# Batch 1 of a fused attention and GELU kernel: v loaded in three lots, a different split of the second GEMM, and the last head pair masked by matmuls

## Chip, cores and metric

The kernel runs on one core of a Trainium2 chip. The metric is the device time of one execution in microseconds (us), the median of the runs shown. In the profile PE is TensorE (matmul), PEld its weight loads, DVE VectorE, ACT ScalarE, POOL GpSimd and SP SyncE, which here only issues transfers.

## What is computed

For 8 batches of 8 heads, with 576 tokens and a head size of 64, the kernel computes causal attention with a decay taken from f, and passes the result through two GEMMs with an exact GELU between them. Cut to what matters, the reference is:

```
scores = scale * q @ k.T
cum    = cumsum(log(clip(f, 1e-4, 1)))
attn   = softmax(where(causal, -1e9, scores + cum[:, None] - cum[None, :]))
x      = (attn @ v) as [4608 tokens, 512]
out    = gelu(x @ w_in[512, 2048]) @ w_out[2048, 512]
```

The inputs are float32 in memory; the transfers that POOL issues turn q, k, w_in and w_out into bf16 on their way.

## The kernel before

One batch is one stage. Its attention handles four head pairs (`HP = 4`), and each pair four score tiles, `scores(b, i, t)` for t = 0 to 3 (L280). A tile is made by PE in one of two PSUM buffers (`s_psum`), turned into `e` by an exponential on ACT (L310), and then its diagonal blocks are made causal. There are two ways for that. With `on_pe` false, POOL writes zeros with an `affine_select` (L312), after the exponential. With `on_pe` true, PE adds a large negative number beforehand by small matmuls of two constants, `key_of` and `after` (L300). Batch 0 and pair 0 of batch 1 go by PE, all others by POOL. Then `attend` (L324) multiplies `e` with the weighted v, `normalize` (L339) divides on DVE, and after transposes to `xT` the first GEMM of this batch (`gemm1`, L381) runs over 16 blocks of d_ff with a GELU on ACT for each (L406).

The second GEMM of batch b lies inside the attention of batch b + 1: it is a generator of single steps, and `take(fill, n)` draws n of them between the attention's instructions on PE. A step for one of 16 blocks kt of d_ff is either one matmul over all 128 rows ("n") or two over 64 rows each into two PSUM banks ("r"), which DVE adds later. For batch 0 there are two parts. `gemm2_first` (L510), 16 steps, lies in the attention of batch 1: token blocks 0 and 1 with kt 0 to 7, so with the first half of w_out. The rest lies in the attention of batch 2: `gemm2_second` (L533) for the same blocks with kt 8 to 15, then `PLAN_0` (L452) for token blocks 2 and 3 with all kt, then batch 1's own second GEMM (`PLAN_1`). PSUM banks come from three pools of two buffers each, "s" for scores, "o" for attention results and transposes, "m" for GEMMs.

There is no scheduler: every engine works its instructions in the order of the program text. So the place of a call sets its place in each engine's queue, that of a transfer too. What matters here:

- POOL issues the transfers of q, k (L108), w_in (L172) and w_out (L176) and also computes: selects (L312), the weighted v (`weigh_v`, L269 and L276), and the copies `behind` and `gate` (L573, L568), which read a tile that a transfer fills and so hold POOL, and all transfers behind it, until that has landed.
- SP issues v (L120), the transposing transfers of q and k for batches 2 and on (`transpose_dma`, L236), those of x (L370), and the stores (L506). A small `memset` of v_sb on POOL ahead of a load of v holds the load until POOL is there.
- w_out comes in four quarters of four kt each (`load_w_out(0)` to `(3)`).

In batch 1, `second_attention` (L721) writes out the order by hand: q and k of pairs 1 to 3 are transposed by PE (`transposes`, L730, and DVE copies L217) right after the first two score tiles, and v of batch 1 comes in two lots of four heads. v and q, k of batch 2 are loaded during batch 1; DVE puts the transposed q and k in their places (`untangle`, L241) during batch 1's first GEMM.

The functions that the diff touches, with the profile's line numbers:

Of the kernel before, what the change touches and what calls it, by code (L numbers as in the profile page):

```python
# [9 lines left out]
FP32 = mybir.dt.float32  # L10
BF16 = mybir.dt.bfloat16
Act = mybir.ActivationFunctionType
Alu = mybir.AluOpType
PSUM = bass.MemoryType.PSUM

P = 128
# [37 lines left out]
def kernel(  # L54
# [223 lines left out]
    e_of = {}  # L278

    def scores(b, i, t):  # L280
        on_pe = b == 0 or (b == 1 and i == 0)
        st = s_psum.tile([P, 2, 512], FP32, tag="s", name=f"s{t}")
        c = 0
        for n, q0, w in STILES[t]:
# [164 lines left out]
        (3, "s", 16 * "n"),  # L449
    ]  # L450

    PLAN_0 = [(2, "o", 16 * "r"), (3, "m", 14 * "r" + 2 * "n")]  # L452
    PLAN_1 = [
        (0, "m", 14 * "r" + 2 * "n"),
        (1, "m", 14 * "r" + 2 * "n"),
# [53 lines left out]

    def gemm2_first(c):  # L510

        pss = [
            m_psum.tile([P, d_model], FP32, tag="m", name="ps2") for _ in range(2)
        ]
        for kq in (0, 4):
            for ts in range(2):
                for kt in range(kq, kq + 4):
                    nc.tensor.matmul(  # L518
                        pss[ts],
                        g_of[c][kt][:, ts * P : (ts + 1) * P],  # L520
                        w_out_sb[:, kt, :],
                        start=(kt == 0),
                        stop=(kt == 7),
                    )
                    if kt == 7:
                        ot_of.append(
                            o_pool.tile([P, d_model], FP32, tag="ot", name="ot")
                        )
                        copy = nc.scalar.copy if ts else nc.vector.tensor_copy
                        copy(ot_of[ts], pss[ts])  # L530
                    yield

    def gemm2_second(c):  # L533

        for ts, pool, tag in ((0, o_psum, "o"), (1, m_psum, "m")):
            banks = [
                pool.tile([P, d_model], FP32, tag=tag, name="ps2") for _ in range(2)
            ]
            for kt in range(8, n_ff):
                for r in range(2):  # L540
                    rows = slice(r * D, (r + 1) * D)
                    nc.tensor.matmul(  # L542
                        banks[r],
                        g_of[c][kt][rows, ts * P : (ts + 1) * P],
                        w_out_sb[rows, kt, :],
                        start=(kt == 8),
                        stop=(kt == n_ff - 1),
                    )
                if kt == n_ff - 1:
                    nc.vector.tensor_tensor(ot_of[ts], ot_of[ts], banks[1], Alu.add)  # L550
                    sum_out(c, ts, ot_of[ts], banks[0])
                yield

    def gemm2_third():
        yield from gemm2_second(0)
        yield from gemm2_rows(0, PLAN_0)
        yield from gemm2_rows(1, PLAN_1)

    def take(gen, n):
# [15 lines left out]
    def first_attention():  # L575
# [45 lines left out]
        weigh_v(0, 3)  # L621
        load_w_in(2)
        nc.gpsimd.memset(v_sb[:, :, 0, 0:1], 0.0)
        load_v(1, 0, 4)
        load_w_in(3)
        load_qk_tokens(1, 0, 4)
        load_qk_tokens(1, 4, 8)
# [93 lines left out]
    def second_attention():  # L721


        b, fill = 1, gemm2_first(0)

        def av(i, h):
            attend(b, i, h, (0, 1, 2, 3, 4))
            normalize(b, i, h)

        def transposes(i, pool, tag):  # L730
            for which in range(2):
                transposes_first(b, i, which, pool, tag)


        nc.scalar.activation(warm[0:1, 0:1], warm[0:1, 0:1], Act.Exp)
        def tiles(i, t):
            scores(b, i, t)
            scores(b, i, t + 1)

        def run(i):  # L740
            av(i, 0)
            av(i, 1)

        tiles(0, 0)
        transposes(1, o_psum, "o")
        transposes(2, m_psum, "m")
        transposes(3, o_psum, "o")
        tiles(0, 2)
        take(fill, 2)
        tiles(1, 0)  # L750
        run(0)
        tiles(1, 2)
        take(fill, 4)
        weigh_v(1, 2)
        tiles(2, 0)
        run(1)
        weigh_v(1, 3)
        tiles(2, 2)
        take(fill, 4)
        tiles(3, 0)  # L760
        transpose_dma(2, 0, 4)
        transpose_dma(2, 4, 8)
        to_xT(b, 0, nc.vector.tensor_copy, o_psum, "o")
        to_xT(b, 1, nc.vector.tensor_copy, o_psum, "o")
        take(fill, 2)
        tiles(3, 2)
        behind(qk_of[2][1], H - 1)
        load_w_out(2)
        load_w_out(3)
        run(2)  # L770
        take(fill, 4)
        av(3, 0)
        both = s_psum.tile([P, 2, 1024], BF16, tag="s", name="ps_x2")
        to_xT(b, 2, nc.scalar.copy, ps=both[:, 0, 0:XC])
        av(3, 1)
        gemm1_begin(1, both)
        x_tail(1)
        load_v(2)

    for b in range(B):  # L780
# [8 lines left out]
        for ffb in range(4 if b < 2 else 5, n_ff):  # L789
            gemm1(b, ffb, ps=spare() if b > 1 and ffb in (7, 8) else None)  # L790
            if b == 0:
# [2 lines left out]
                        transposes_first(1, 0, which, o_psum, "o")  # L794
                if ffb == 12:
                    behind(qk_of[1][0], H - 1)
                    nc.gpsimd.memset(v_sb[:, 4:8, 0, 0:1], 0.0)
                    load_v(1, 4, 8)
                    weigh_v(1, 0)
                    load_w_out(1)  # L800
                    weigh_v(1, 1)
                    load_qk_tokens(2)
            elif b + 1 < B:
                first, gap = (5, 3) if b == 1 else (1, 4)
                at, late = divmod(ffb - first, gap)
# [40 lines left out]
```

## Time and profile before

| what | value |
|---|---|
| median of 5 runs | 337.94 us (337.22 to 340.28) |
| the profiled execution's own time | 339.24 us |
| its span, first to last instruction | 337.1 us |
| time outside the span | 2.1 us |
| PE busy | 324.0 us, 96% of the span |
| ACT busy | 209.3 us, 62% |
| DVE busy | 181.1 us, 54% |
| POOL busy | 122.6 us, 36% |
| granted TensorE clock | 0.995 of full |
| attention of batch 1, by the timeline | 40.6 to 57.5 us |
| first GEMM of batch 1, by the timeline | 57.6 to 72.0 us |
| attention of batch 2, by the timeline | 72.0 to 103.4 us |

Times in windows and timelines are in us from the start of the span. A timeline row gives start, length, engine, line, operation, output and inputs, and in brackets the idle time of the engine ahead of it with what ended it. A windows row gives the stretch, its length, then for PE, PEld, DVE, ACT and POOL the busy time with the number of instructions, the granted clock, the busy share of the 16 DMA engines (packets can overlap, so that it can pass 1), and GB/s. In the DMA view, a queue's row gives its packets, MB, and the time its packets took as a share of the 16 engines: q0 carries the transfers that POOL issues, q1 those of SP.

### The profile page before, as it was taken

To read this page: it belongs to the slowest core of one execution; us is meant where nothing else is said; L and a number is where in the kernel's file an instruction comes from. 1 tells how busy PE (TensorE), PEld (TensorE's weight loads), DVE (VectorE), ACT (ScalarE), POOL (GpSimd) and SP (SyncE) were. 2 spreads that over 40 slices of the span, in tenths; PEclk is the share of its full clock that TensorE was granted. 3 is DMA by queue.
4 is the path that set the end of the run, shared out by engine and by line. 5 is a ranking of instruction groups with operands and counts; after the bars stand their busy time and mean duration, and the time that the engine had idled before them with its cause. 6 is when DMAs were issued, how large, how long until landed. Compare 5 with 4: busy or idle time off the path is not lost.

```text
span 337.1 us, 7780 instructions
## 1 busy us (share of the span) xinstructions
PE 324.0 (96%) x3121; PEld 172.3 (51%) x3161; DVE 181.1 (54%) x414; ACT 209.3 (62%) x299; POOL 122.6 (36%) x250
## 2 busy tenths in 40 slices
PE   8699989999999999999999999999999999999995
PEld 3584555445554456445654555446544654444443
DVE  4761265674466945895479547964696540020011
ACT  6967698673653788278927982788368855404600
POOL 8191098009436134633554243724361420000000
PEclk9989999999999999999999999999999999999999
DMA  7999999997998989697958697599810241011013
GB/s 116 183 137 185 196 190 171 153 182 144 210 221 181 138 167 202 120 140 130 211 148 128 123 198 150 94 151 210 146 56 2 82 61 64 0 63 64 0 39 86
DMA packets 104627, 44.16 MB, mean 131 GB/s; under 512 B 83408, under 2 KB 100048, under 8 KB 104592
## 3 DMA queue, kind: packets, MB, share of 16 engines
q1 hardware_dynamic: 87296, 29.52, 45.9%
q0 software_dynamic: 16896, 13.63, 27.9%
q8 instruction: 24, 0.39, 0.5%
q10 hardware_dynamic: 400, 0.52, 0.4%
q14 instruction: 11, 0.09, 0.1%
HBM read 36.85 MB, written 9.44 MB: 137 GB/s over the span
## 4 chain that ended last, share of the span: by engine, by line
PE 90%; issue 2%; SPq 2%; DVE 1%; POOL 1%; ACT 1%; DMA 1%; POOLq 0%; ACTq 0%; DVEq 0%
PE ps L386 36%; PE ps L482 26%; PE o L331 10%; PE ps L422 8%; PE s L300 7%; SPq L120 2%; ACT e L310 1%; PE ps L542 1%; DMA v_sb<-in_v_dram 1%; POOL q L108 1%; PE ps_x L364 1%; PE ps L518 0%; POOL k L108 0%; DVE qT L217 0%; DVE kT L217 0%
## 5 line engine op out<-in xcount | busy, mean ns | idle before, releaser
L406 ACT ACTIVATE g<-ps 128x512 bf16<-128x512 f32 x144 | 82.1, 601 | 83.6 <-PE ps L386 83.6
L310 ACT ACTIVATE e<-s 128x896 bf16<-128x896 f32 (+2 forms) x128 | 100.2, 835 | 22.7 <-PE s L300 17.5
L386 PE MATMUL ps<-xT,w_in_sb 128*128 128x512 bf16 x497 | 111.5, 379 | 0.7
L482 PE MATMUL ps<-w_out_sb,g 64*128 64x512 bf16 (+1 forms) x692 | 104.4, 376 | 1.6 <-issue 1.3
L386 PEld LDWEIGHTS <-w_in_sb 128*128 128x128 bf16 x576 | 56.0, 98 | 67.5 <-issue 1.8
L312 POOL TENSOR_SCALAR_AFFINE_SELECT e<-e 128x256 bf16<-128x256 bf16 (+1 forms) x135 | 49.1, 383 | 86.1 <-ACT e L310 85.7
L482 PEld LDWEIGHTS <-g 64*128 64x128 bf16 (+1 forms) x711 | 39.4, 95 | 34.8 <-issue 4.2
L269 POOL TENSOR_TENSOR vw<-v_sb,wT 128x640 bf16<-128x640 f32 x30 | 38.6, 1289 | 27.6 <-DMA v_sb<-in_v_dram 15.4
L300 PE MATMUL s<-qT,kT 64*128 64x320 bf16 (+4 forms) x384 | 44.2, 278 | 2.9 <-ACT e L310 1.9
L250 DVE COPY kT<-tk 64x288 bf16<-64x288 bf16 x96 | 43.9, 457 | 1.6
L250 DVE COPY qT<-tq 64x288 bf16<-64x288 bf16 x96 | 38.7, 403 | 5.1 <-DMA tq<-q 3.7
L331 PE MATMUL o<-vw,e 128*128 128x65 bf16 x960 | 38.1, 195 | 2.0 <-DVE vw L269 1.2
L331 PEld LDWEIGHTS <-e 128*128 128x128 bf16 x960 | 35.1, 99 | 9.4 <-issue 2.7
L490 DVE COPY ot<-ps 128x512 f32<-128x512 f32 x20 | 13.8, 692 | 47.1 <-PE ps L482 47.1
L345 DVE TENSOR_TENSOR x<-o,r 128x320 bf16<-128x320 f32 x64 | 31.4, 491 | 3.6 <-DMA xT<-x 1.4
L300 PEld LDWEIGHTS <-kT 64*128 64x128 bf16 x384 | 19.8, 94 | 24.6 <-issue 8.1
L431 DVE COPY ot<-ps 128x512 f32<-128x512 f32 (+2 forms) x9 | 5.7, 632 | 49.6 <-PE ps L422 49.6
L422 PE MATMUL ps<-w_out_sb,g 128*128 128x512 bf16 (+2 forms) x142 | 27.9, 355 | 0.1
L422 PEld LDWEIGHTS <-g 128*128 128x128 bf16 x144 | 13.5, 98 | 14.5
L344 DVE RECIPROCAL r<-o 128x5 f32<-128x5 f32 x64 | 12.1, 189 | 13.3 <-PE o L331 13.2
L502 DVE TENSOR_TENSOR ot<-ot,ps 128x512 f32<-128x512 f32 x22 | 15.1, 685 | 1.1
L386 PE MATMUL ps<-tails,w_in_sb 128*128 128x512 bf16 x63 | 14.2, 377 | 0.1
(69 smaller groups left out, 138.3 us busy)
## 6 DMA issues: line engine op xcount, KB each, us to landing
out_dram<-ot SPq DMA_DIRECT2D x32, 256.0 KB, 2.5
v_sb<-in_v_dram SPq DMA_DIRECT2D x24, 256.0 KB, 4.9
q<-in_q_dram POOLq DMA_DIRECT2D x6, 576.0 KB, 6.4
k<-in_k_dram POOLq DMA_DIRECT2D x6, 576.0 KB, 8.5
v_sb<-in_v_dram SPq DMA_DIRECT2D x22, 128.0 KB, 4.8
w_in_sb<-in_moe_w_in_dram POOLq DMA_DIRECT2D x4, 512.0 KB, 8.4
w_out_sb<-in_moe_w_out_dram POOLq DMA_DIRECT2D x4, 512.0 KB, 10.0
q<-in_q_dram POOLq DMA_DIRECT2D x4, 144.0 KB, 4.0
```

What stands on the lines that cost most here:

```text
L250: nc.vector.tensor_copy(rows[:, odd], src[odd * D : (odd + 1) * D, 2 * i + h].rearrange("d j p -> d p j"),)
L269: eng.tensor_tensor(vw(b)[:, hs, :, 0:D], v_sb[:, hs, :, :], w.unsqueeze(3).to_broadcast([P, 2, NBLK, D]), Alu.mult,)
L300: nc.tensor.matmul(to, *ab, start=half < 0, stop=half == 1 or not masked)
L310: nc.scalar.activation(et[:, :, z:c], st[:, :, z:c], Act.Exp, scale=scale)
L312: nc.gpsimd.affine_select(out=et[:, :, c0 + z : c0 + P], in_=et[:, :, c0 + z : c0 + P], compare_op=Alu.is_ge, fill=0.0, base=z, pattern=[[ ...
L331: nc.tensor.matmul(o[:, m, :], e_of[b, i, t][:, h, c : c + P], vw_of[b][:, 2 * i + h, n, :], start=(n == 0), stop=(n == m),)
L345: nc.vector.tensor_tensor(x_of[b, i][:, :, h, :], o[:, :, 0:D], r.unsqueeze(2).to_broadcast([P, NBLK, D]), Alu.mult,)
L386: nc.tensor.matmul(ps, w_in_sb[:, kt, ffb * P : (ffb + 1) * P], src[:, kt, 0:TC], start=(kt == 0), stop=(kt == n_dm - 1),)
L406: nc.scalar.activation(g_of[c][ffb], ps, Act.Gelu)
L422: nc.tensor.matmul(pss[ts][:, c0:c1], g_of[c][kt][:, ts * P : (ts + 1) * P], w_out_sb[:, kt, c0:c1], start=(kt == 0), stop=(kt == n_ff - 1),)
L482: nc.tensor.matmul(banks[r], g_of[c][kt][rows, ts * P : (ts + 1) * P], w_out_sb[rows, kt, :], start=kt == (steps.index("r") if r else 0), ...
L502: nc.vector.tensor_tensor(ot, ot, bank, Alu.add)
```

## The change

It touches batch 1 and what lies around it, in five places.

1. v of batch 1 comes in three lots: heads 0 and 1 early, in the place of heads 0 to 3, and heads 2 and 3, then 4 to 7, behind the gate on q.
2. The transfer of k for batch 2 goes from the first GEMM of batch 0 to the attention of batch 1, and that of w_out's second quarter to a place behind the gate on that k, where quarters 2 and 3 are already.
3. `gemm2_first` takes all four token blocks with kt 0 to 3, so with w_out's first quarter alone; `gemm2_second` takes the other 12 kt of all four blocks, and `PLAN_0` is gone. The number of steps stays 16 in batch 1 and 112 in batch 2.
4. Pair 3 of batch 1 is masked by PE.
5. In batch 1's attention the transposes of pairs 1 and 2 change their PSUM pools, two steps of the second GEMM go ahead of score tiles 2 and 3 of pair 0, the transposes of pair 3 behind these, and two steps fewer are drawn ahead of pair 3's `attend`.

```diff
--- before.py
+++ after.py
@@ -278,7 +278,7 @@
     e_of = {}
 
     def scores(b, i, t):
-        on_pe = b == 0 or (b == 1 and i == 0)
+        on_pe = b == 0 or (b == 1 and i in (0, HP - 1))
         st = s_psum.tile([P, 2, 512], FP32, tag="s", name=f"s{t}")
         c = 0
         for n, q0, w in STILES[t]:
@@ -449,7 +449,6 @@
         (3, "s", 16 * "n"),
     ]
 
-    PLAN_0 = [(2, "o", 16 * "r"), (3, "m", 14 * "r" + 2 * "n")]
     PLAN_1 = [
         (0, "m", 14 * "r" + 2 * "n"),
         (1, "m", 14 * "r" + 2 * "n"),
@@ -509,51 +508,55 @@
 
     def gemm2_first(c):
 
-        pss = [
-            m_psum.tile([P, d_model], FP32, tag="m", name="ps2") for _ in range(2)
-        ]
-        for kq in (0, 4):
-            for ts in range(2):
-                for kt in range(kq, kq + 4):
+        for two in (0, 2):
+            pss = [
+                m_psum.tile([P, d_model], FP32, tag="m", name="ps2") for _ in range(2)
+            ]
+            for ts in (two, two + 1):
+                for kt in range(n_ff // 4):
                     nc.tensor.matmul(
-                        pss[ts],
+                        pss[ts - two],
                         g_of[c][kt][:, ts * P : (ts + 1) * P],
                         w_out_sb[:, kt, :],
                         start=(kt == 0),
-                        stop=(kt == 7),
+                        stop=(kt == n_ff // 4 - 1),
                     )
-                    if kt == 7:
+                    if kt == n_ff // 4 - 1:
                         ot_of.append(
                             o_pool.tile([P, d_model], FP32, tag="ot", name="ot")
                         )
-                        copy = nc.scalar.copy if ts else nc.vector.tensor_copy
-                        copy(ot_of[ts], pss[ts])
+                        copy = nc.scalar.copy if ts == 3 else nc.vector.tensor_copy
+                        copy(ot_of[ts], pss[ts - two])
                     yield
 
     def gemm2_second(c):
 
-        for ts, pool, tag in ((0, o_psum, "o"), (1, m_psum, "m")):
+        kts = range(n_ff // 4, n_ff)
+        for ts in range(n_sub):
+            pool, tag = ((o_psum, "o"), (m_psum, "m"))[ts % 2]
+            steps = "r" * len(kts) if ts < 3 else "r" * (len(kts) - 2) + "nn"
             banks = [
                 pool.tile([P, d_model], FP32, tag=tag, name="ps2") for _ in range(2)
             ]
-            for kt in range(8, n_ff):
-                for r in range(2):
-                    rows = slice(r * D, (r + 1) * D)
+            for kt, step in zip(kts, steps):
+                last = kt == kts[steps.rfind("r")]
+                for r in range(2 if step == "r" else 1):
+                    rows = slice(r * D, (r + 1) * D) if step == "r" else slice(0, P)
                     nc.tensor.matmul(
                         banks[r],
                         g_of[c][kt][rows, ts * P : (ts + 1) * P],
                         w_out_sb[rows, kt, :],
-                        start=(kt == 8),
-                        stop=(kt == n_ff - 1),
+                        start=(kt == kts[0]),
+                        stop=last if r else kt == n_ff - 1,
                     )
+                if last:
+                    nc.vector.tensor_tensor(ot_of[ts], ot_of[ts], banks[1], Alu.add)
                 if kt == n_ff - 1:
-                    nc.vector.tensor_tensor(ot_of[ts], ot_of[ts], banks[1], Alu.add)
                     sum_out(c, ts, ot_of[ts], banks[0])
                 yield
 
     def gemm2_third():
         yield from gemm2_second(0)
-        yield from gemm2_rows(0, PLAN_0)
         yield from gemm2_rows(1, PLAN_1)
 
     def take(gen, n):
@@ -621,7 +624,7 @@
         weigh_v(0, 3)
         load_w_in(2)
         nc.gpsimd.memset(v_sb[:, :, 0, 0:1], 0.0)
-        load_v(1, 0, 4)
+        load_v(1, 0, 2)
         load_w_in(3)
         load_qk_tokens(1, 0, 4)
         load_qk_tokens(1, 4, 8)
@@ -742,15 +745,17 @@
             av(i, 1)
 
         tiles(0, 0)
-        transposes(1, o_psum, "o")
-        transposes(2, m_psum, "m")
+        transposes(1, m_psum, "m")
+        transposes(2, o_psum, "o")
+        take(fill, 2)
+        tiles(0, 2)
         transposes(3, o_psum, "o")
-        tiles(0, 2)
         take(fill, 2)
         tiles(1, 0)
         run(0)
         tiles(1, 2)
         take(fill, 4)
+        load_qk_tokens(2, which="k")
         weigh_v(1, 2)
         tiles(2, 0)
         run(1)
@@ -765,10 +770,11 @@
         take(fill, 2)
         tiles(3, 2)
         behind(qk_of[2][1], H - 1)
+        load_w_out(1)
         load_w_out(2)
         load_w_out(3)
         run(2)
-        take(fill, 4)
+        take(fill, 2)
         av(3, 0)
         both = s_psum.tile([P, 2, 1024], BF16, tag="s", name="ps_x2")
         to_xT(b, 2, nc.scalar.copy, ps=both[:, 0, 0:XC])
@@ -794,12 +800,12 @@
                         transposes_first(1, 0, which, o_psum, "o")
                 if ffb == 12:
                     behind(qk_of[1][0], H - 1)
-                    nc.gpsimd.memset(v_sb[:, 4:8, 0, 0:1], 0.0)
+                    nc.gpsimd.memset(v_sb[:, 2:8, 0, 0:1], 0.0)
+                    load_v(1, 2, 4)
                     load_v(1, 4, 8)
                     weigh_v(1, 0)
-                    load_w_out(1)
                     weigh_v(1, 1)
-                    load_qk_tokens(2)
+                    load_qk_tokens(2, which="q")
             elif b + 1 < B:
                 first, gap = (5, 3) if b == 1 else (1, 4)
                 at, late = divmod(ffb - first, gap)
```

## Prediction

> **What bounds the kernel now.** I read the page first (PE busy for 96% of the span), then busy time by stretch around batch 1, the chain that ended last, and the timelines of POOL and PE.
>
> The stretches are batch 1's attention up to its last exponential, its tail, and its first GEMM:
>
> ```profile
> 40.20:55.80 15.60, 13.75 (x250) 8.97 (x253) 9.03 (x20) 14.39 (x19) 12.82 (x25) 1.00 1.19 195
> 55.80:58.80 3.00, 3.00 (x47) 2.00 (x46) 2.06 (x7) 2.10 (x4) 2.04 (x4) 1.00 0.89 134
> 58.80:72.00 13.20, 13.10 (x64) 5.84 (x65) 8.86 (x27) 9.09 (x16) 0.42 (x1) 1.00 1.25 175
> ```
>
> Only in the first does PE (first number behind the length) stand still: 1.85 us. ACT (fourth) fills 14.39 of 15.60 us there, so that stretch is set by ACT; the others by PE. The clock is full. So all that a better order in batch 1 can win is some of 1.85 us, and ACT gives up 1.2 at most. The chain, in us from the start, with lengths:
>
> ```profile
> 41.72 0.76 DVE qT L217
> 42.48 0.68 DVE kT L217
> 43.16 0.04 issue
> 43.20 0.45 PE ps_f L208 x12
> 43.64 0.40 PE s L300 x6
> ...
> 55.67 0.81 PE ps L518 x3
> 56.48 0.47 PE o L331 x15
> ```
>
> Pair 3's transposes wait for DVE to free their banks, and the scores behind them come late: exponential (0,2) starts at 44.12, though its predecessor ended at 43.91. In the tail four steps of the second GEMM (L518) lie ahead of pair 3's attend. Then batch 2:
>
> ```profile
> 75.44 1.28 POOL L269 TENSOR_TENSOR vw<-v_sb,wT 128x640 bf16<-128x640 f32 x1 [15.38 <-DMA v_sb<-in_v_dram]
> ...
> 78.18 0.83 POOL L108 DMA_DIRECT2D q<-in_q_dram  x1
> 79.01 0.77 POOL L108 DMA_DIRECT2D k<-in_k_dram  x1
> 79.79 1.72 POOL L312 TENSOR_SCALAR_AFFINE_SELECT e<-e 128x256 bf16<-128x256 bf16 x5
> ```
> ```profile
> 83.47 1.11 PE L331 MATMUL o<-vw,e 128*128 128x65 bf16 x30
> ```
>
> POOL waits 15 us for v of batch 2, which lands at 75.27 as the last of a long row of transfers. Everything behind it on POOL follows without a gap, up to the selects of batch 2's pair 0, done at 81.51. PE uses the last of them some 0.15 us into its attend at 83.47. This cover of about 2.1 us is what the change can use up.
>
> **The change, part by part.** The sum is made against the profiled span, 337.1 us.
>
> *Order at the head.* With the first two steps ahead of score tile (0,2), the bank comes free with DVE's copy at 42.48, the steps take 2 x 0.216 (start to start of L518), and tile (0,2) starts at 43.26, when exponential (0,0) has freed its buffer, instead of 43.58. Its exponential starts at 43.83: 0.29 us earlier. But pair 3's transposes (0.54) and two more steps (0.43) now stand between tile (0,3), which waits for exponential (0,1) as before, and tile (1,0): that starts near 45.37, not 45.09, and its exponential at 45.83, not 45.56. Behind attend of pair 0 this evens out to 0.1 us earlier. The steps need w_out's first quarter by 42.53; it landed at 44.06. With 320 KB less of v ahead (at 190 GB/s, 1.7 us) it lands near 42.4. If it came as late as before, tile (0,2) would start at 44.5 and its exponential 0.9 us later than before.
>
> The order adds two passages between full-row and half-row matmuls. The trace's last step before pair 3's tile starts at 53.51 and the tile at 53.83, 0.10 above the step's 0.216; both passages lie where PE waits for ACT and I take nothing more for them. The Trainium skill ("TensorEngine Tiling (Array Packing)", Key Properties) says against this change that every change of tiling mode drains TensorE. It gives no figure; by the trace's 0.10 the rule would cost two passages 0.2 us if nothing covered them.
>
> *Pair 3's mask.* It adds 18 matmuls on PE and removes five selects on POOL (0.29 to 0.41 us each, 1.9 in all). The same masks in pair 0 move tile 0's end from 0.37 to 0.53 us and take 0.08 in each of tiles 2 and 3 and 0.03 in tile 1: 0.35 us. At (3,0) ACT already waited for PE (0.17), so this 0.16 shows: its exponential starts at about 52.67, 0.09 later than before. The last select (55.87 to 56.27) goes, but PE had a step to do until 56.32 anyway.
>
> *Steps of the second GEMM.* Two steps leave the tail: -0.43 us of PE, where PE is bound. With the 0.3 that the masks and the late head leave, attend of pair 3 starts near 56.2 instead of 56.32. I take **-0.15 us** for batch 1's attention; bounds +0.9 (w_out as late as before) and -0.6 (exponentials without the gaps of 0.21, 0.31 and 0.09). In batch 2 the number of steps is the same; DVE gets two more adds of 0.69 us, beside 26 us in which it is busy 13.9, in banks that PE wants again 12 steps (2.6 us) later: nothing.
>
> *k of batch 2.* Its issue (0.77 us of POOL) moves from 46.4 to behind the select of tile (1,3), 49.3. Queued behind it on POOL: weighing v for pairs 2 and 3, and the selects of pair 2, which end at 54.7 instead of 54.18; attend of pair 2 starts at 54.6 and wants the last at 54.7: nothing. A q of this size, 576 KB, issued at 78.18 landed 6.68 us later; k then lands at about 56 to 57, before at 55.63. SP's first transpose of k, and on POOL the gate with all of w_out, follow by 0 to 1.3 us; I take 0.7.
>
> *w_out's second quarter.* It was moved at 43.4 to 49.1; now it goes behind the gate, ahead of the other two. Its own date is no trouble: wanted at 72.2, it lands near 65; the last quarter, wanted at 74, near 71. But it shares the DMA engines with the transposes and with v of batch 2. Packets of the two queues while both have work (32 to 38 us), of w_out alone (46.5 to 48.5), and of SP's alone (69 to 74):
>
> ```profile
> q0 software_dynamic: 1155, 0.86, 91.1%
> q1 hardware_dynamic: 1156, 0.29, 36.4%
> ```
> ```profile
> q0 software_dynamic: 400, 0.40, 123.4%
> ```
> ```profile
> q1 hardware_dynamic: 4535, 1.14, 134.2%
> ```
>
> Sharing is packet for packet, though w_out's are 1 KB and SP's 256 B. A quarter is 512 packets; alone, at 200 per us, that is 2.6 us. From 60 to 74.4 us the engines hardly pause, so v of batch 2 lands 2.6 us later for the quarter and 0.7 for the gate: 78.5. (The skill, "DMA: Bandwidth & Descriptors", states that each engine takes the queues in turn by packets, but of many descriptors each; if that meant turns by bytes, v would suffer less. The rows above are even by the trace's packets, and I go by them.) Between the ends (v not later at all, if the quarter fits into the pauses at 56 to 60 and 61.5 to 63; v 5 us later, if it takes the 3.4 us of the shared rate, 610 packets in 4 us, plus the gate's 1.3), I take **3.2 us**.
>
> *The cover in batch 2.* POOL's chain moves by 3.2; pair 0's last select ends at 84.7. PE, 0.15 earlier, wants it at 83.45. **PE waits 1.2 us.** Pair 1's selects then end near 89.2; PE is there at about 89.9, so it doesn't wait twice. DVE's `untangle`, behind the later transposes, ends near 77 instead of 74.14, and adds that free banks wait behind it; PE wants those at 77.65 and could stop 0.5 to 0.9 us there. That is part of the 1.2, not on top, since a PE that comes later waits less for the select.
>
> **Sum:** -0.15 + 1.2 = +1.05, so a span of 338.1 us. The time outside the span (339.24 - 337.1 = 2.1) doesn't change. The profiled run was 1.3 us over the median of 337.94; I add the difference to the median and, as the 0.7 of the gate is the weakest term, take 0.9: **338.8 us**.
>
> **Rivals.**
> *A, not slower: v of batch 2 lands within the cover.* If the quarter falls largely into the pauses of the DMA, or k lands by 55.6 so that the gate, with no selects ahead of it, opens half a us sooner than 56.2, v is late by less than 2.1 us, PE waits for nothing, and batch 1's -0.15 (to -0.6) remains: 337.8, down to 337.3. For it: DMA rows 56 to 58.5 show no packet of w_out. Against: they come there from the issue's own delay, which the new order has too.
> *B, clearly slower: the transfers pile up.* From a delay of v of about 4 us on, PE's wait passes 2 us. At 5 us POOL's last select of pair 0 ends at 86.5: PE waits 3.0, 337.94 + 2.9 = 340.8. For it: single packets between 58.5 and 63 took up to 1.3 us, and the queue is longer now. Against: v has the engines alone at the end, at 900 packets per us.
> *C, faster beyond what I see:* all idle time of batch 1's attention gone, 336.1. ACT's load speaks against it.
>
> **How the numbers follow.** A measurement of this kernel tells about 0.5% (1.7 us) from no change. Forecast (v 2.2 to 4 us late, 338 to 339.6): 0.55. A: 0.23. B: 0.18. C: 0.04. The range leaves out C and the upper half of B: 337.2 to 340.5. Within 0.5% lie the forecast and A: 0.78; slower, B: 0.18; faster, C: 0.04.
>
> **What would show it.** POOL's wait for v of batch 2 (L269) ends near 78.5 instead of 75.44, and PE shows an idle time ahead of L331 near 83.5, ended by POOL's select. Attend of pair 3 in batch 1 starts near 56.2. k of batch 2 lands at 56 to 57. If the wait ends before 77.4, A holds; if batch 1's stretch changes by over 0.6 us, my reading of its ACT bound is wrong.

## The result, and the profile after

The changed kernel takes 340.26 us (median of 44 runs, 338.31 to 344.92), and the kernel before, run beside it on the same chips, 338.0 us (79 runs). The ratio is **1.0057, 95% interval 1.0044 to 1.0069**: 1.9 us more (1.5 to 2.3). Two of the 44 executions of the changed kernel (343.59 and 344.92 us) fell in a slower state with a lower granted clock and are left out of the ratio; without them its median is 340.0. The forecast had 0.9 us more. The time lies in the range, near its upper end, and just past the 0.5% that I had set for telling a change at all.

The profiled execution of the changed kernel took 340.49 us, 0.2 over its median, with a span of 338.6. For before there are two profiles by now: the one of the prediction (own time 339.24, span 337.1), and another of the unchanged kernel, taken with the experiments (own time 337.09, span 335.0). I call it *before, second profile*. The two stand 1.2 over and 0.9 under the median of 338.0, and the reason is in batch 0: in the first, PE paused for 1.2 us and the TensorE clock fell for 3.4 us behind that (shown at the end), and batch 1 began at 40.58 us; in the second, without the fall, at 38.29. The stages of batches 1 to 6 are equal in both to 0.01 us. In the changed kernel batch 1 began at 38.80 with a full clock. So I compare it with the second profile, stage by stage, and keep in mind that 0.9 us of the whole difference is that profile's luck.

| stage (length in us, from PE's first instruction of it to that of the next) | before, 1st profile | before, 2nd profile | after | after less 2nd |
|---|---|---|---|---|
| start of batch 1's attention | 40.58 | 38.29 | 38.80 | +0.51 |
| batch 1, attention | 16.97 | 16.97 | 17.70 | +0.73 |
| batch 2, attention | 31.45 | 31.46 | 32.16 | +0.70 |
| batch 2, first GEMM | 13.91 | 13.91 | 14.65 | +0.74 |
| batch 4, first GEMM | 13.91 | 13.91 | 14.78 | +0.87 |

These make 3.55 of the 3.6 us between the spans. (In batch 1 of after, the record of one matmul is missing; its first GEMM is put at 56.5.)

From the page of the changed kernel, the span, the engines' busy times, and the chain that ended last:

```profile
span 338.6 us, 7819 instructions
...
PE 323.9 (96%) x3139; PEld 171.6 (51%) x3179; DVE 182.9 (54%) x416; ACT 209.3 (62%) x299; POOL 120.4 (36%) x245
...
PE 72%; DMA 8%; SPq 7%; issue 5%; POOL 4%; DVE 1%; ACT 0%; POOLq 0%; DVEq 0%; ACTq 0%
PE ps L386 28%; PE ps L481 22%; PE ps L422 8%; PE o L331 8%; PE s L300 6%; SPq L120 4%; DMA v_sb<-in_v_dram 4%; SPq L236 3%; DMA xT<-x 2%; DMA k<-in_k_dram 2%; POOL vw L269 1%; POOL q L108 1%; POOL e L312 1%; POOL k L108 1%; DVE x L345 0%
```

PE's busy time hardly says anything: 323.9 us, against 324.0 in the first profile of before. What changed is who leads: 91% of the chain was PE in the second profile of before, 72% now, and SP's queue, the transfers of v and POOL have taken the rest. The chain around batch 2's first attend, in order of time:

```profile
71.52 5.30 DMA v_sb<-in_v_dram
...
77.16 1.28 POOL vw L269
78.44 0.17 POOL vw L276
78.61 1.21 POOL vw L269
79.82 0.17 POOL vw L276
79.99 0.76 POOL q L108
80.75 0.77 POOL k L108
81.51 1.73 POOL e L312 x5
83.24 0.05 issue
83.29 0.71 PE o L331 x17
```

This is the row of POOL's work that the prediction followed: the last part of v lands at 76.82, POOL weighs it, issues q and k of batch 3, and makes the five selects of pair 0; PE is released at 83.29. The attend itself began at 82.43, 11.51 us after batch 2's first score, as in before, and ran into the wait:

```profile
82.43 0.23 PE L331 MATMUL o<-vw,e 128*128 128x65 bf16 x2
82.94 1.32 PE L331 MATMUL o<-vw,e 128*128 128x65 bf16 x28 [0.28 <-POOL e L312]
```

Its 30 matmuls take 1.83 us here, 1.11 in before. The places where PE stood still for a transfer, from its timelines in batches 1, 2 and 4:

```profile
41.68 0.39 PE L517 MATMUL ps<-w_out_sb,g 128*128 128x512 bf16 x1 [1.01 <-DMA w_out_sb<-in_moe_w_out_dram]
...
104.69 2.10 PE L386 MATMUL ps<-xT,w_in_sb 128*128 128x512 bf16 x9 [0.58 <-DMA xT<-x]
...
175.19 13.11 PE L386 MATMUL ps<-xT,w_in_sb 128*128 128x512 bf16 x58 [0.70 <-DMA xT<-x]
```

None of the three was in my sum. The first I had held to be just avoided; the other two lie in first GEMMs, where I had not looked. The stretches of the prediction, cut at the same places of the work:

```profile
38.42:54.83 16.41, 14.25 (x270) 9.16 (x272) 10.35 (x22) 14.36 (x19) 10.15 (x20) 1.00 0.95 156
54.83:57.83 3.00, 2.95 (x46) 1.94 (x46) 2.19 (x7) 2.17 (x4) 2.49 (x4) 1.00 0.89 107
57.83:70.92 13.09, 13.04 (x63) 5.72 (x61) 7.00 (x21) 9.02 (x16) 0.42 (x1) 1.00 1.20 197
```

Batch 1's attention up to its last exponential grew from 15.60 to 16.41 us, though ACT has no more to do in it (14.36 us, 14.39 before) and POOL less.

### The profile page after: what moved, and what is told of

It reads as the page before. It is cut to its first block, busy times and chain, and to the rows that moved or that the text cites. A ratio compares the mean times of both kernels' runs of the same rounds, so it can differ in the third digit from the quotient of the medians.

```text
span 338.6 us, 7819 instructions
## 1 busy us (share of the span) xinstructions
PE 323.9 (96%) x3139; PEld 171.6 (51%) x3179; DVE 182.9 (54%) x416; ACT 209.3 (62%) x299; POOL 120.4 (36%) x245
## 4 chain that ended last, share of the span: by engine, by line
PE 72%; DMA 8%; SPq 7%; issue 5%; POOL 4%; DVE 1%; ACT 0%; POOLq 0%; DVEq 0%; ACTq 0%
PE ps L386 28%; PE ps L481 22%; PE ps L422 8%; PE o L331 8%; PE s L300 6%; SPq L120 4%; DMA v_sb<-in_v_dram 4%; SPq L236 3%; DMA xT<-x 2%; DMA k<-in_k_dram 2%; POOL vw L269 1%; POOL q L108 1%; POOL e L312 1%; POOL k L108 1%; DVE x L345 0%
## 5 line engine op out<-in xcount | busy, mean ns | idle before, releaser
L481 PE MATMUL ps<-w_out_sb,g 64*128 64x512 bf16 (+1 forms) x631 | 96.9, 376 | 1.4 <-issue 1.1
L312 POOL TENSOR_SCALAR_AFFINE_SELECT e<-e 128x256 bf16<-128x256 bf16 (+1 forms) x130 | 47.1, 383 | 82.7 <-ACT e L310 82.5
L481 PEld LDWEIGHTS <-g 64*128 64x128 bf16 (+1 forms) x649 | 36.4, 95 | 31.3 <-issue 3.8
L250 DVE COPY kT<-tk 64x288 bf16<-64x288 bf16 x96 | 43.1, 449 | 4.4 <-DMA tk<-k 2.9
L250 DVE COPY qT<-tq 64x288 bf16<-64x288 bf16 x96 | 39.7, 413 | 4.1 <-DMA tq<-q 2.7
L489 DVE COPY ot<-ps 128x512 f32<-128x512 f32 x18 | 12.5, 692 | 44.6 <-PE ps L481 44.6
```

The costliest lines, as they stand in the source:

```text
L250: nc.vector.tensor_copy(rows[:, odd], src[odd * D : (odd + 1) * D, 2 * i + h].rearrange("d j p -> d p j"),)
L312: nc.gpsimd.affine_select(out=et[:, :, c0 + z : c0 + P], in_=et[:, :, c0 + z : c0 + P], compare_op=Alu.is_ge, fill=0.0, base=z, pattern=[[ ...
L481: nc.tensor.matmul(banks[r], g_of[c][kt][rows, ts * P : (ts + 1) * P], w_out_sb[rows, kt, :], start=kt == (steps.index("r") if r else 0), ...
```

## The experiments

Two theories at the start. **Mine:** the loss is in batch 2, and it is the late transfers: w_out's second quarter and k put v of batch 2 behind the cover. **The rivals:** the loss is batch 1's new order; or it is the mask's 36 additional instructions on PE, which are seen in batch 4. Twelve kernels were run, each timed against before beside it, but for one that is before itself. Edits are relative to the changed kernel, where nothing else is said. "W" stands for w_out's second quarter.

| run | kernel | ratio to before (95%) | batch 1 att. | batch 2 att. | batch 2 GEMM | batch 4 GEMM |
|---|---|---|---|---|---|---|
| | before, 2nd profile | | 16.97 | 31.46 | 13.91 | 13.91 |
| | the change | 1.0057 (1.0044-1.0069) | 17.70 | 32.16 | 14.65 | 14.78 |
| e1 | W back to its early place | 1.0073 (1.0044-1.0102) | 18.68 | 31.46 | 13.91 | 15.06 |
| e2 | W and k back | 1.0095 (1.0058-1.0132) | 18.79 | 31.45 | 13.91 | 14.54 |
| e3 | v of batch 1 in two lots | 1.0089 (1.0055-1.0122) | 20.39 | 32.22 | 14.70 | 14.29 |
| e4 | the head's order back | 1.0057 (1.0024-1.0091) | 17.22 | 31.77 | 15.24 | 14.37 |
| e5 | pair 3 masked by POOL | 1.0068 (1.0037-1.0100) | 17.36 | 32.68 | 15.21 | 13.91 |
| e6 | before + 36 PE instructions | 0.9995 (0.9969-1.0021) | 17.41 | 31.46 | 13.91 | 14.09 |
| e7 | W ahead of the gate | 1.0160 (1.0110-1.0211) | 17.61 | 35.67 | 14.78 | 14.51 |
| e9 | before + new split + mask | 1.0035 (1.0005-1.0065) | 20.19 | 31.46 | 13.91 | 14.59 |
| e10 | before + new split, W late | 1.0024 (0.9998-1.0050) | 17.06 | 33.32 | 14.74 | 13.91 |
| e11 | before + new split, k late | 1.0009 (0.9981-1.0037) | 17.06 | 31.45 | 13.91 | 13.91 |
| e12 | before + new split, both late | 1.0056 (1.0025-1.0087) | 17.47 | 32.81 | 14.06 | 13.91 |

The lengths in us are each from one profiled execution; the ratios are from all runs. The two need not agree to half a us. (Outside the columns, e4 lost another 0.84 us in batch 3's first GEMM.)

### e1 and e2: w_out's second quarter back early, without and with k

```diff
         behind(qk_of[2][1], H - 1)
-        load_w_out(1)
         load_w_out(2)
...
                     weigh_v(1, 0)
+                    load_w_out(1)
                     weigh_v(1, 1)
```

e2 has besides this `load_qk_tokens(2)` whole in its old place.

> The changed kernel, with only the transfer of w_out's second quarter put back to its old place in batch 0's first GEMM. My theory (the quarter delays v of batch 2, and so POOL's selects and the attend of batch 2's pair 0, and later x of batch 2): v of batch 2 lands 2 to 2.6 us earlier against PE, PE's waits in batch 2 (0.7 us at its first attend and 0.7 us at its first GEMM in the changed kernel's profile) go, and the ratio to before falls from 1.006 to about 1.002. Rival 1 (the loss is the wait for w_out's first quarter in batch 1, 1.0 us in that profile): ratio stays within 0.001 of 1.006. Rival 2 (the loss comes from the later k of batch 2): stays too, and v of batch 2 is as late as in the changed kernel.

> As the run before, and k of batch 2 is also issued with q again, so that POOL's transfers stand in the old order. My theory: as the run before, 1.002, since k landed no later in the changed kernel (55.21 us) than before (55.63). Rival 2 (the later k): only here does the ratio fall, to about 1.002, and the run before stays at 1.006.

The two waits of batch 2 went as my theory said: attention 31.46 and 31.45, first GEMM 13.91 in both. The time did not. In batch 1 of e1 PE now waits for POOL twice (in e2 as well, 0.69 and 0.71 us); first PE's timeline, then POOL's:

```profile
48.14 0.24 PE L331 MATMUL o<-vw,e 128*128 128x65 bf16 x2 [0.47 <-POOL e L312]
49.08 1.32 PE L331 MATMUL o<-vw,e 128*128 128x65 bf16 x28 [0.71 <-POOL e L312]
```
```profile
45.45 1.27 POOL L269 TENSOR_TENSOR vw<-v_sb,wT 128x640 bf16<-128x640 f32 x1 [6.48 <-DMA v_sb<-in_v_dram]
46.68 0.22 POOL L276 CAST vw<-wT 128x10 bf16<-128x10 f32 x1
46.82 0.83 POOL L108 DMA_DIRECT2D q<-in_q_dram  x1
47.66 1.72 POOL L312 TENSOR_SCALAR_AFFINE_SELECT e<-e 128x256 bf16<-128x256 bf16 x5
```

The second lot of v landed at 45.28 beside W, which landed at 45.59; POOL could weigh heads 2 and 3 only at 45.45, and pair 1's selects stood behind that and behind the issue of q. So the parts of the change seem to lean on each other: v in three lots, with heads 2 and 3 behind the gate, comes in time only when W is out of the way, and W's going costs batch 2. What e1 and e2 show is the cause of batch 2's waits; they don't give it a price.

### e3, e4, e5: one part undone each

```diff
-        load_v(1, 0, 2)
+        load_v(1, 0, 4)
...
-                    nc.gpsimd.memset(v_sb[:, 2:8, 0, 0:1], 0.0)
-                    load_v(1, 2, 4)
+                    nc.gpsimd.memset(v_sb[:, 4:8, 0, 0:1], 0.0)
```
```diff
-        transposes(1, m_psum, "m")
-        transposes(2, o_psum, "o")
-        take(fill, 2)
-        tiles(0, 2)
+        transposes(1, o_psum, "o")
+        transposes(2, m_psum, "m")
         transposes(3, o_psum, "o")
+        tiles(0, 2)
...
         run(2)
-        take(fill, 2)
+        take(fill, 4)
         av(3, 0)
```
```diff
-        on_pe = b == 0 or (b == 1 and i in (0, HP - 1))
+        on_pe = b == 0 or (b == 1 and i == 0)
```

> The changed kernel, with v of batch 1 in two lots of four heads again. If the early first quarter of w_out is what the smaller first lot buys, it lands 1.7 us later, near 43.3 us, and the first two steps of the second GEMM, which now stand ahead of score tile 2, hold PE 1.7 us longer: ratio 1.011. Rival (v's lots only change POOL's own waits): 1.006, and PE's wait ahead of the first step stays at 1.0 us.

> The changed kernel, with the old order of transposes, steps and score tiles at the head of batch 1 and four steps again ahead of pair 3's attend. Theory that the head's order costs time because PE stands at the first step until w_out's first quarter has landed (1.0 us): the first step comes 1.8 us later, the wait goes, two steps (0.43 us) come back at the tail: 0.3 to 0.6 us less than the changed kernel, ratio 1.004 to 1.005. Rival (ACT sets batch 1, a wait of PE there costs nothing): 0.2 to 0.4 us more than the changed kernel, 1.007.

> The changed kernel, with pair 3 of batch 1 masked by POOL again, so with 36 instructions fewer on PE. In the changed kernel's profile PE also waits 0.9 us at the first GEMM of batch 4, far from the change, for an x transfer that is held up while 16 KB of code are fetched (172.3 us; before, the fetch came at 173.7, behind that transfer). Theory 'code': the 36 instructions put PE's code fetches where they meet that transfer; without them, the first GEMM of batch 4 takes 13.9 us again instead of 14.8, and the ratio falls by 0.002. Rival 'mask on PE': the mask's 0.35 us shorten batch 1's attention by up to 0.3 us and batch 4 keeps its 14.5 to 15 us. Rival 'chance': batch 4's wait comes and goes in every kernel.

e3 makes the wait for w_out's first quarter worse, which three lots were to prevent: 1.97 us at 42.44, and the clock fell behind it. Its ratio lies between that of the theory (1.011) and that of the rival (1.006). e4 takes 0.5 us out of batch 1, and e5 takes the whole wait out of batch 4 and 0.3 us out of batch 1. The latter is not the mask's doing alone, since w_out's first quarter landed in time in e5. Neither kernel is faster than the change by its ratio, though a gain had been expected of both. Their profiles have 1.3 us more than before in batch 2's first GEMM, the change 0.7. Whether that is chance of one execution I can't tell.

### e6: before with 36 more instructions on PE

```diff
-        warm_up(9)
+        warm_up(27, 171)
```

`warm_up(n, w)` makes n matmuls of w columns on PE ahead of batch 0; 27 of 171 columns take as long as nine of 512, and each brings a matmul and a weight load: 36 instructions more, as many as the mask's 18 matmuls bring.

> The kernel before, whose nine warm-up matmuls of 512 columns are 27 of 171 columns: the same columns, and 36 instructions more on PE, as the mask adds. Theory 'code': its code fetches fall as in the changed kernel, the first GEMM of batch 4 takes 14.5 to 15 us instead of 13.9, and the kernel is 0.5 to 0.9 us slower than before, ratio 1.002. Rival 'chance': 13.9 us and ratio 1.000.

In the second profile of before the trace's instruction queue moves 24 packets of 16 KB, while PE works 6282 matmuls and weight loads, so one for about 260 of them; I take these packets for PE's code. With 36 instructions more, the packet that comes at 171.4 us there comes at 170.2, while the x of batch 4 is being transposed: that transfer took 4.29 us instead of 2.62, and the first GEMM 0.18 more. The place was as expected, the size less than expected (0.5 to 0.9), because PE comes to that part of x only 0.86 us into the GEMM. By the ratio nothing is lost. In all eight kernels with the 36 instructions (the change, e1 to e4, e6, e7, e9) batch 4's first GEMM is longer than 13.91, by 0.2 to 1.2; in the six without (before twice, e5, e10 to e12) it is 13.91.

### e7: w_out's second quarter ahead of the gate

```diff
-        behind(qk_of[2][1], H - 1)
         load_w_out(1)
+        behind(qk_of[2][1], H - 1)
         load_w_out(2)
```

> The changed kernel, with w_out's second quarter issued ahead of the gate on k of batch 2 instead of behind it; POOL stood idle there for 1.85 us. My theory (the quarter pushes v of batch 2, and with it PE's first attend and first GEMM of batch 2): v of batch 2 lands 1 to 2 us earlier, the two waits of 0.7 us in batch 2 shrink to 0 to 0.4 each, ratio 1.002 to 1.004. It takes nothing from v of batch 1, as the first of these runs did by putting the quarter far ahead. Rival (the transfers' total sets v of batch 2, not where the quarter stands): no change, 1.006.

My theory fell here in its simple form, and the rival with it: less of a queue behind the gate was to help, and the kernel became 1.6% slower, with batch 2's attention 4.2 us longer. Two rows of PE's timeline of e7, then the two queues in the DMA view from 60 to 63 us:

```profile
78.81 0.37 PE L545 MATMUL ps<-w_out_sb,g 64*128 64x512 bf16 x1 [2.15 <-DVE ot L553]
...
86.14 1.32 PE L331 MATMUL o<-vw,e 128*128 128x65 bf16 x28 [0.71 <-POOL e L312]
```
```profile
q1 hardware_dynamic: 227, 0.06, 78.5%
q0 software_dynamic: 113, 0.11, 67.0%
```

W was issued at 52.85 and landed at 60.03, with the third quarter (issued at 54.22) right behind it, so that w_out ran together with the transposing transfers of q and k earlier than elsewhere. From 60 to 63 us both all but stood: 340 packets in 3 us, when w_out alone had moved 200 per us. The first transposed k landed at 66.83 (58.1 to 64.1 in the others), v of batch 2 at 80.03. DVE's untangling came so late that PE waited 2.15 us for a bank behind it: the second wait of the prediction, which it put at 0.5 to 0.9 us.

### e8 and e9: before again, and before with the new split and the mask

e8 is the kernel before, unchanged: the second profile. e9 is before with the new `gemm2_first` and `gemm2_second` and the mask; loads and order are before's.

```diff
-        on_pe = b == 0 or (b == 1 and i == 0)
+        on_pe = b == 0 or (b == 1 and i in (0, HP - 1))
```

> The kernel before, for a second profile. In the first one the granted clock fell to 0.81 from 16.9 to 25.1 us, behind a wait of 1.2 us for the first v, and stayed full in the changed kernel's. If that is chance of the one execution and worth about 1.8 us at the start of batch 1, a profile with a full clock starts batch 1's scores near 38.8 us instead of 40.6, and ends near 335.5 to 336.5 if nothing later takes it back (336.5 if batch 1's steps then wait for w_out's first quarter, as in the changed kernel).

> The kernel before with two parts of the change alone: the split of the second GEMM by quarters and pair 3's mask on PE. All transfers and the order at batch 1's head stand as before. My theory: v of batch 2 lands as in the second profile of before (34 us after batch 1's first score), PE waits neither at batch 2's first attend (stage 31.45 us) nor at its first GEMM (13.91); the mask costs batch 1 0.2 to 0.3 us, and its 36 instructions bring the code fetch of 16 KB onto batch 4's x transfer (first GEMM of batch 4 14.1 to 15 us). Ratio 1.001 to 1.003. Rival (the split itself costs, by its two more adds on DVE): batch 2's attention 31.8 us or more with no wait for POOL.

e9 has none of batch 2's waits. Its profiled execution, at 341.29 us the slowest of its twelve, lost in batch 1, where w_out's first quarter landed at 44.48, PE waited 2.12 us for it and the clock fell behind that. Its runs are 0.35% slower than before (0.05 to 0.65%). Whether that wait is there in most of them, one profile can't tell.

### e10, e11, e12: before with the new split, and one late transfer, or both

Relative to e9: pair 3 masked by POOL again, and in e10 the first, in e11 the second of these two edits, in e12 both (in e11 and e12 the old call loads q alone).

```diff
         behind(qk_of[2][1], H - 1)
+        load_w_out(1)
         load_w_out(2)
...
                     weigh_v(1, 0)
-                    load_w_out(1)
                     weigh_v(1, 1)
```
```diff
         take(fill, 4)
+        load_qk_tokens(2, which="k")
         weigh_v(1, 2)
...
-                    load_qk_tokens(2)
+                    load_qk_tokens(2, which="q")
```

> The kernel before with the split of the second GEMM, and w_out's second quarter behind the gate on k of batch 2; k is issued early as before, pair 3 is masked by POOL. My theory of the prediction: the quarter alone makes v of batch 2 2.6 us later (36.7 us after batch 1's first score); the cover in the second profile of before is 2.7 us, so PE waits 0 to 0.3 us at batch 2's first attend, and batch 2's first GEMM may wait a few tenths: ratio 1.000 to 1.002. Rival (the engines take much longer for the quarter when they share it with the transposes): v lands at 38 us or later and the ratio is 1.004 or more.

> As the run before, with k of batch 2 late as in the changed kernel and w_out's second quarter early as before. My theory: the gate opens 1.4 to 1.6 us later against batch 1's first score (k lands at 16.4 us after it, not 14.8), v of batch 2 lands 1.5 us later (35.6), within the cover: no wait in batch 2, ratio 1.000. Rival: the later k is what costs, ratio 1.003 or more.

> As the two runs before, with both late as in the changed kernel. My theory: the two delays add (v of batch 2 at 38 us after batch 1's first score, as in the changed kernel) and pass the cover of 2.7 us by 1.3: PE waits 1 to 1.5 us at batch 2's first attend, and 0.7 us or so at batch 2's first GEMM, because SP's chain of v of batch 3, q and k and x behind it is late too: ratio 1.005 to 1.007, nearly the whole loss of the change. Rival (batch 1's own waits, w_out's first quarter above all, are the loss): ratio up to 1.003.

**Both transfers late, with nothing else of the change but the split, cost 0.56% (0.25 to 0.87), as much as the whole change.** Late k alone, and so the split too, costs nothing that the runs can tell (0.09%, -0.19 to 0.37), as expected: v comes 1.3 us later, within the cover, and PE doesn't pause in batch 2's attention, as the stretch in e11 shows (length, then PE's busy time):

```profile
69.98:101.50 31.52, 31.52 (x367) 16.57 (x367) 17.06 (x39) 16.45 (x19) 15.79 (x32) 1.00 1.04 183
```

Late W alone put v 4.6 us later in its profile, not 2.6: the rival in e10's expectation had that size right (38 us or later; it was 38.7), and PE waited 1.9 us in the attention and 0.8 in the first GEMM. But e10's runs have a median of only 0.24% over before; its profiled execution, 340.26 us, was 1.4 over that. So I suppose that how late v comes differs from execution to execution; one profile can't show it. The delays don't add up either: e12 has v 4.5 us later, no more than e10. And e12 lost only 0.15 us in batch 2's first GEMM, where 0.7 had been expected. The intervals of e10, e11 and e12 overlap, so whether W alone carries the loss stays open.

## Why the prediction was right or wrong

**The late quarter and k: right in the sum, not in its terms.** v of batch 2 was to land 3.2 us later; counted from batch 1's first score it landed 38.02 us after it, against 34.69 in the first profile of before (3.3 more) and 34.11 in the second (3.9 more). k landed at 55.21, 16.4 after the first score, where 56 to 57 (15.4 to 16.4) had been forecast. The terms were 2.6 for the quarter and 0.7 for the gate. Counted against the first profile, late k alone made it 0.8 (e11), the late quarter alone 4.0 (e10), and both 3.9 (e12). So the gate's term was right, the quarter's too small in e10, and that the two added up to the measured 3.3 is in part luck. The prediction had also named a date: if POOL's wait ended before 77.4, rival A would hold. It ended at 77.16, but in an execution whose batch 1 began 1.8 us earlier; counted from the first score, 77.4 is 36.8, and it ended at 38.4.

**The cover: right.** PE was to wait 1.2 us at the attend, ended by POOL's select; it lost 0.70 there, ended by that select. The difference is batch 1: I had PE 0.15 earlier, it came 0.73 later, and so used 0.73 of the 3.3 itself. 3.33 - 0.73 - 2.0 (the cover by the profiles) is 0.6. That the cover is what counts can be read from the profiles. Here are eight of the fourteen: v's landing less batch 2's first score, and what PE's time in batch 2's attention has over 31.46:

| | e8 | before | e1 | e11 | after | e12 | e10 | e7 |
|---|---|---|---|---|---|---|---|---|
| v lands after batch 2's first score, us | 2.73 | 3.31 | 3.82 | 3.98 | 5.90 | 6.72 | 7.24 | 9.41 |
| PE's loss, us | 0 | 0 | 0 | 0 | 0.70 | 1.35 | 1.86 | 4.21 |

Up to 4 us nothing, then about a us for each: the cover ends near 5.3 us, 2.0 past the first profile of before and 2.6 past the second. I had 2.1. The other six fall into the same line: e9, e2 and e6 (1.27, 2.34 and 2.45) lose nothing, e4, e3 and e5 (5.50, 6.13 and 6.42) lose 0.31, 0.76 and 1.22.

**What I did not carry on: the next stage. This failed.** "PE waits 1.2 us" was to be the whole price of batch 2. But the late POOL also issues q and k of batch 3 late, and there a new pile begins. k of batch 3 was issued at 80.73 in after and landed at 91.79; in the second profile of before it was issued at 76.14 and landed at 85.65. SP loads v of batch 3 meanwhile. The DMA queues from 86.7 to 92 us in after, and from 85 to 90 in the second profile of before, while these loads are issued:

```profile
q1 hardware_dynamic: 1353, 0.60, 70.7%
q0 software_dynamic: 667, 0.50, 60.6%
```
```profile
q1 hardware_dynamic: 3011, 0.93, 122.2%
q0 software_dynamic: 24, 0.01, 1.9%
```

In before POOL's transfers were over when v began. Now 667 of their packets are in the way, SP moves less than half as many, and its third load of v is through only at 92.07, 0.3 us after k has landed. The transposes of q, k and x behind it on SP come late, and PE waits for x in batch 2's first GEMM: 0.74 us. The link from k to SP's third load rests on times alone, but they recur in all fourteen profiles: in the nine in which k was still on its way when that load was begun, its issue took 2.6 to 3.7 us and was through 0.1 to 0.4 us after k's landing; in the other five it took 0.9 to 1.4. The loss goes with it: where the load was through 11.6 us or more ahead of batch 2's first GEMM, nothing was lost there; 11.25 ahead (e12) 0.15 us; 11.0 to 10.2 ahead, 0.7 to 1.3.

**The order at the head: wrong, and w_out's first quarter with it.** The forecast for batch 1 was -0.15 us, with bounds of +0.9 and -0.6; it was +0.73, and the prediction had called a change of over 0.6 the sign that its reading of ACT's bound is wrong. The exponentials show where; ACT's timelines of the second profile of before (first score at 38.29), e7 (38.82; it has the change's order, and there w_out's first quarter landed in time), and after (38.80):

```profile
41.85 3.05 ACT L310 ACTIVATE e<-s 128x896 bf16<-128x896 f32 x4 [0.21 <-PE s L300]
...
46.94 3.17 ACT L310 ACTIVATE e<-s 128x896 bf16<-128x896 f32 x4 [0.23 <-ACT e L310]
50.29 3.22 ACT L310 ACTIVATE e<-s 128x896 bf16<-128x896 f32 x4 [0.18 <-PE s L300]
```
```profile
44.18 3.03 ACT L310 ACTIVATE e<-s 128x896 bf16<-128x896 f32 x4 [0.60 <-PE s L300]
47.84 3.02 ACT L310 ACTIVATE e<-s 128x896 bf16<-128x896 f32 x4 [0.63 <-PE s L300]
51.36 2.59 ACT L310 ACTIVATE e<-s 128x896 bf16<-128x896 f32 x3 [0.50 <-PE s L300]
```
```profile
42.77 1.51 ACT L310 ACTIVATE e<-s 128x896 bf16<-128x896 f32 x2 [0.63 <-PE s L300]
44.46 3.18 ACT L310 ACTIVATE e<-s 128x896 bf16<-128x896 f32 x4 [0.18 <-PE s L300]
48.13 3.02 ACT L310 ACTIVATE e<-s 128x896 bf16<-128x896 f32 x4 [0.49 <-PE s L300]
51.65 2.59 ACT L310 ACTIVATE e<-s 128x896 bf16<-128x896 f32 x3 [0.50 <-PE s L300]
```

Counted from the first score, the first exponential of pair 2 starts at 46.94 - 38.29 = 8.65 us in before, 9.02 in e7, 9.33 in after; that of pair 3 at 12.00, 12.54, 12.85. So the first steps of my working hold: in e7 tile (0,2)'s exponential is 0.30 us earlier, as forecast (0.29), and tile (1,0)'s 0.37 later (forecast 0.27). What failed is the next sentence, "Behind attend of pair 0 this evens out": the 0.37 stay to the end, since ACT waits for PE's scores half a us and more once per pair and never catches up. So ACT does not set this stretch alone: it was busy for the same 14.4 us in a stretch that is 0.8 longer. e4, with the old order, has all exponentials up to pair 3 where before has them. With before's order, too, a delay at this place stays: in e6 and e12 PE stood 0.63 and 0.69 us for w_out's first quarter, and batch 1 is 0.44 and 0.50 us longer. That first quarter, landing late, adds 0.3 in after. The mask adds 0.17 at pair 3 (forecast 0.16; e4 shows it alone), and the tail gives 0.1 back, of a forecast 0.43. That is 0.37 + 0.31 + 0.17 - 0.1 = 0.75.

The quarter: I put its landing at 42.4, that is 1.8 us after batch 1's first score. It landed 1.5 to 2.1 us after it in e1, e2, e4, e5 and e7, and 2.84 in after; with v in two lots, 3.4 to 5.9 (e3, e6, e9 to e12; before itself 2.9 and 3.5). So "just in time" was right in the mean, and the three lots do what they are for; a margin of 0.1 us was only too small to count on. The sum had even less: the lot is smaller by 288 KB (576 rows of 256 B for each of two heads), not 320, which at 190 GB/s is 1.55 us and a landing at 42.5. I also had written "The clock is full", which is so from 40.2 us on. In the row of the clock on the page the third digit is an 8, and I passed over it: that execution's batch 1 began 1.8 to 2.3 us late. The sum took little harm from it: counted from batch 1's first score, its transfers landed 0.2 to 0.6 us later than in the second profile (k 15.05 and 14.84, v 34.69 and 34.11, w_out's first quarter 3.48 and 2.89).

**The mask: its price was right, its side effect not in the sum.** The 36 instructions move what I take for PE's code fetches, and batch 4 loses 0.87 us in after. By the ratios of e5 and e6 that has no weight that the runs can tell.

**The rivals.** A is ruled out: v did not land within the cover. B is nearer in the total than its place suggests: v came 3.9 us later than in the second profile, but the loss was spread over three places instead of 2.9 us at one. The number of the forecast came near in part by luck: of the five stages that differ in the profiles, one, batch 2's attention, had been forecast with its sign and cause.

**What stays open.** The spans of the two profiles differ by 3.6 us, the runs by 1.9. 0.9 is the second profile's luck. Part of that luck shows: neither profile of before waits for w_out's first quarter in batch 1, but four of the other five kernels with its two lots of v and its order, e6, e9, e10 and e12, wait 0.63, 2.12, 0.29 and 0.69 us for it. So the 0.73 of batch 1 is a difference to a good case. For the rest I have only that single executions differ by 1 to 2 us, as e10's did. Undone alone, no part makes the change faster, and no kernel here beats before: without the late transfers (e1, e2) batch 1 loses what batch 2 wins.

## What to carry to other kernels

When a transfer moves behind another, follow the delay past the wait that it causes: whoever was held (here POOL) issues the next stage's transfers late, and these run into a queue that they had kept clear of. A pause that ends just in time in one profile should be counted with the spread of the landing, here more than a us, and not with its margin. Before taking a stretch as the base of a sum, look along the row of the granted clock over all that precedes it; a dip there lengthens the span that the sum starts from.

## What the runs showed of the hardware

**The clock can fall after a short pause.** PE's windows in the first profile of before; behind PE, PEld, DVE, ACT and POOL stands the granted clock:

```profile
13.40:16.87 3.47, 1.88 (x46) 1.35 (x41) 2.40 (x4) 3.22 (x5) 0.86 (x2) 0.95 0.74 161
16.87:20.30 3.43, 3.43 (x56) 2.80 (x56) 2.05 (x5) 0.85 (x2) 3.37 (x4) 0.55 0.58 81
20.30:25.06 4.76, 4.76 (x121) 4.15 (x118) 3.57 (x11) 4.12 (x6) 4.76 (x8) 1.00 1.18 178
```

PE was busy for 1.88 of 3.47 us, its longest pause being 1.23. Windows cut more finely put the clock at 0.50 from 16.54 to 19.95, so for 3.41 us, and full before and behind that; the 0.95 and 0.55 are means. The same, 3.41 us at 0.50, followed pauses of 1.97 us (e3, from 42.56 on) and 2.12 us (e9, from 45.56 on). It did not follow the pause of 2.15 us in e7, with PE busy for 1.66 of 3.80 us ahead of it, nor that of 1.01 in after. The Trainium skill ("TensorE: Matmul & The Clock Gate", Part 1: The HAM clock gate) states that the clock halves after an idle window of about 3.4 us and comes back after a busy one, the window running free of the kernel. The length and depth of the dip agree with the three profiles; that a whole window must be idle does not.

**Transposing transfers and w_out's can all but stop when they come together**: 340 packets in 3 us in e7 (227 of SP's queue, 113 of POOL's), and 40 from 62 to 63 us in the first profile of before. It passes: from 63 to 68 us of the changed kernel, while both were still under way, the two queues moved 778 and 777, packet for packet as the prediction had it. What begins and ends the slow part no run shows.

**What seems to be a code fetch can slow a transfer that lies beside it**: x of batch 4 in 4.29 us (e6) and 4.97 us (after) instead of 2.62. The kernels with and without the 36 instructions show that these decide it; that the packets are code, and that they are what slows x, is read from sizes and times alone.
